# The last of 64 work units as eight block products, and closing sums moved to other places

## The chip, the cores and the metric

The kernel runs on one core of a Trainium2 chip. The metric is device time in microseconds (us) from start to end of one execution. The engines named below are PE (TensorE, matrix products into PSUM), DVE (VectorE), ACT (ScalarE), POOL (GpSimd) and SP (the engine that issues nearly all transfers). Each engine runs its own instructions strictly in program order and waits on semaphores for the others.

## The reference

```
def attention(q, k, v, p):                      # 8 batches, 8 heads, 576 tokens, width 64; p: 32 rows
    packed = softmax(p @ k.T / 8) @ v
    return softmax(q @ packed.T / 8) @ packed
x = attention(...).transpose(0, 2, 1, 3).reshape(4608, 512)
p = domain_probs / (domain_probs.sum(-1, keepdims=True) + 1e-9)
for e in range(4):                              # w1[e] 512x1024, w2[e] 1024x512, all fp32
    out += p[:, e:e+1] * (relu(x @ w1[e]) @ w2[e])
```

## The kernel before, in words

The second matrix product, `h @ w2`, is what this change is about. The 4 experts of 1024 hidden rows are cut into 8 chunks of 512, and the tokens into 8 batches of 576. One chunk of one batch is a unit: 64 units, counted here from 0. Batches go in pairs; within a pair the chunks go 0 to 7 and the two batches alternate, so unit 61 is chunk 6 of batch 7, unit 62 chunk 7 of batch 6 and unit 63, the last, chunk 7 of batch 7.

Within a unit the hidden block is a 2x2 matrix of blocks: a11, a12, a21, a22 (first digit token half, second digit hidden half), the weights are blocks b11 to b22 (hidden half, output half), and the product is formed in Winograd's way with seven block products instead of eight. `ORDER` lists their left operands, a11, s3, s1, s2, a22, s4, a12, where s1 to s4 are sums of the a blocks; the right operands (b11, b21, b22 and the sums t1 to t4) were formed once and are kept in DRAM (`td`), from which tiles `tt` come back. Every operand is split into a rounded high part and a low part, and a block product is 12 matmuls of 128x128 by 288 columns (`product`, L527): three of high and low for each of two hidden tiles and two output tiles. The first matmul of a product already reads the low part of its left operand.

- `mm1_group` (L414): four groups of 12 matmuls for each unit make the hidden blocks. DVE applies relu and the token weight, and builds s1 to s4 into tiles `sblk` and `ablk`.
- `s_operand` (L464): the split of a left operand into a tile `st` (4 buffers), two products ahead of its use: ACT casts the high part, POOL subtracts the low part. a12 is split by ACT and DVE into `stl`.
- `product`: its PSUM tile `dbl` is then added on DVE to one of seven accumulators `acc0` to `acc6` of the batch (the number is the place in `ORDER`); for chunk 0 ACT copies it.
- `combine` (L584), the closing sums of a batch: seven adds of accumulators, three on DVE, four on POOL, and four stores, one step after each product of the next unit. For the last batch `finish` (L556) does them instead, woven into unit 63's products, all on DVE.
- `g_form` (L370): in the first unit of a pair too, two PSUM tiles of matmuls (line L124) after product 0 make the weights of the next chunk (`ghl`), each tile emptied by two ACT casts and two DVE subtractions.

PSUM holds four `dbl` tiles, handed out in turn to products, groups and `g_form`. The order on TensorE is fixed by hand; the order on DVE, ACT, POOL and SP is chosen when the program is built, by a scheduler, within order constraints (`Behind`, L78, holds some DVE and POOL work behind other work). So the code's place of a step and its place in an engine's queue can differ.

Of the kernel before, what the change touches and what calls it, by code (L numbers as in the profile page):

```python
# [39 lines left out]
def attention_moe(ctx: ExitStack, tc: tile.TileContext, q, k, v, p, dp, w1, w2, out):  # L40
# [91 lines left out]
    def dbl():  # L132
        return ps_dbl.tile([P, 2, 512], F32, name="dbl")
# [15 lines left out]
    def hi_of(dst, src, eng):  # L149
        if eng in (nc.scalar, bact):  # L150
            return eng.copy(out=dst, in_=src)  # L151
        return eng.tensor_copy(out=dst, in_=src)

    def lo_of(dst, src, hi, eng):
        return eng.tensor_tensor(out=dst, in0=src, in1=hi.bitcast(F32), op=ALU.subtract)
# [255 lines left out]

    blocks = {}

    def mm1_group(u, kh, c):  # L414
        sb, ch, b = units[u]
        xh, xl = xs[b]
        ts = slice(c * HS, (c + 1) * HS)
        ps = dbl()
        for fi in range(2):
            f = 2 * kh + fi  # L420
            fs = slice(f * P, (f + 1) * P)
            n = 0
            for g in range(NG):
                ghl = gs[b, ch][g]
                for hl, rx in ((0, xl), (0, xh), (1, xh)):
                    mm(
                        out=ps[:, fi, 0:HS], lhsT=ghl[:, hl, fs], rhs=rx[:, g, c, 0:HS],
                        start=n == 0, stop=n == 3 * NG - 1,
                    )
                    n += 1  # L430
        psv = ps[:, :, 0:HS]

        def held(name):
            tag, bufs = ("ablk", 3) if name[0] == "a" else ("sblk", 4)
            blocks[u, name] = hpool.tile([P, 2, HS], F32, name=tag, bufs=bufs)
            return blocks[u, name]

        def add(dst, x, y, op):
            vec.tensor_tensor(out=dst, in0=x, in1=y, op=op)

        name = f"a{c + 1}{kh + 1}"
        vec.scalar_tensor_tensor(
            out=held(name) if c == kh else psv, in0=psv, scalar=0.0,
            in1=pbt[b][:, ts].rearrange("p (o t) -> p o t", o=1).broadcast_to([P, 2, HS]),
            op0=ALU.max, op1=ALU.mult,
        )
        if name == "a21":
            add(held("s3"), blocks[u, "a11"], psv, ALU.subtract)
            add(psv, psv, blocks[u, "a22"], ALU.add)
            add(held("s2"), psv, blocks[u, "a11"], ALU.subtract)  # L450
            nc.scalar.copy(out=held("s1"), in_=psv)  # L451
            if (u, "a12") in blocks:
                add(held("s4"), blocks[u, "a12"], blocks[u, "s2"], ALU.subtract)
        elif name == "a12":
            if (u, "s2") in blocks:
                add(held("s4"), psv, blocks[u, "s2"], ALU.subtract)
            else:
                blocks[u, "a12"] = psv
            st = hpool.tile([P, 2, 2, HP], F32R, name="stl")[:, :, :, 0:HS]
            hi_of(st[:, 0], psv, nc.scalar)  # L460
            lo_of(st[:, 1], psv, st[:, 0], vec)
            blocks[u, "op", NPROD - 1] = st

    def s_operand(u, i):  # L464

# [61 lines left out]
    def product(u, i):  # L527
        sb, ch, b = units[u]
        st, t = blocks.pop((u, "op", i)), tt[ch, i]
        ps = dbl()  # L530
        for j in range(2):
            n = 0
            for fi in range(2):
                for tl, sl in ((0, 1), (0, 0), (1, 0)):
                    mm(
                        out=ps[:, j, 0:HS], lhsT=t[:, tl, fi, j * P:(j + 1) * P], rhs=st[:, sl, fi, :],
                        start=n == 0, stop=n == 5,
                    )
                    n += 1
        order["product"] = order["free"][-1]  # L540
        psv = ps[:, :, 0:HS]
        if (b, i) not in accs:
            accs[b, i] = apool.tile([P, 2, HS], F32, name=f"acc{i}")
            nc.scalar.copy(out=accs[b, i], in_=psv)  # L544
        elif ch < NCH - 1 or b < B - 1:
            vacc.tensor_tensor(out=accs[b, i], in0=psv, in1=accs[b, i], op=ALU.add)
        else:
            finish(b, ORDER[i], psv)

    def store(b, t, r, n):  # L550
        nc.sync.dma_start(
            out=out[n * DH:(n + 1) * DH, b * S + r * HS:b * S + (r + 1) * HS].rearrange("(j p) t -> p j t", p=P),
            in_=t,
        )

    def finish(b, name, psv):  # L556

        m = {n: accs[b, i] for i, n in enumerate(ORDER)}

        def add(dst, x, y, op=ALU.add):  # L560
            vec.tensor_tensor(out=dst, in0=x, in1=y, op=op)

        t = m[name]
        if name == "a22":
            add(t, m["s3"], t, ALU.subtract)
            add(t, t, psv, ALU.subtract)
            store(b, t, 1, 0)
            return
        add(t, psv, t)
        if name == "a11":  # L570
            add(m["s2"], m["s2"], t)
            add(m["a12"], m["a12"], t)
        elif name == "s2":
            add(m["s3"], m["s3"], t)
            add(m["s4"], m["s4"], t)
            add(m["s4"], m["s4"], m["s1"])
            add(m["s1"], m["s1"], m["s3"])
            store(b, m["s1"], 1, 1)
        elif name == "s4":
            store(b, t, 0, 1)  # L580
        elif name == "a12":
            store(b, t, 0, 0)

    def combine(b):  # L584

        m = {n: accs[b, i] for i, n in enumerate(ORDER)}
        for eng, dst, x, y, op, to in (
            (cvec, "s2", "s2", "a11", ALU.add, None),
            (gq, "a12", "a12", "a11", ALU.add, (0, 0)),
            (cvec, "s3", "s3", "s2", ALU.add, None),  # L590
            (gq, "s4", "s4", "s1", ALU.add, None),
            (gq, "s4", "s4", "s2", ALU.add, (0, 1)),
            (cvec, "s1", "s1", "s3", ALU.add, (1, 1)),
            (gq, "a22", "s3", "a22", ALU.subtract, (1, 0)),
        ):
            eng.tensor_tensor(out=m[dst], in0=m[x], in1=m[y], op=op)
            if to is not None:
                store(b, m[dst], *to)
            yield

# [29 lines left out]
    def drain(gen):  # L630
        for _ in gen:
            pass
# [85 lines left out]
        w2_load(1, kh, raw_tile)  # L718
    tsteps = nothing
    kind = None  # L720
    sums, back = nothing, second_batch()
    for u, (sb, ch, b) in enumerate(units):
        pos = u % (2 * NCH)
        odd = pos % 2 == 1
# [21 lines left out]
        if fch is not None and u != 3 and not (u > 3 and odd):  # L746
            tsteps = t_form(fch)
        form_at = FORM.get(u, () if fch is None else (1, 2, 3, 4) if odd else (1, 4))
        for i in range(NPROD):
            product(u, i)  # L750
            n = i + LA
            if n < NPROD:
                s_operand(u, n)
            elif nxt:
                s_operand(u + 1, n - NPROD)
            if i in gat:
                if gat == (0,):
                    drain(gsteps)
                    if 0 < u < 4:
                        raws = w1_load({1: 0, 2: 2}[u])  # L760
                        if u == 2:
                            gsteps, gat = g_form([0, 1], 2, raws), (4, 5)
                else:
                    next(gsteps, None)
            if nxt:
                for grp in ((GROUPS_FIRST, GROUPS_LATE)[u] if u < 2 else GROUPS).get(i, ()):
                    mm1_group(u + 1, *grp)
            if i == 4 and 2 <= u < len(units) - 2 and units[u + 2][1] % 2 == 0:
                load_probs(units[u + 2][2], units[u + 2][1] // 2)
            if u == 0:  # L770
                next(back, None)
                next(back, None)
            elif i == 5 and kind != "scores" or i == 2 and u > 2 or i == 0 and odd and u > 3:
                kind = next(back, None)
            if i in form_at:
                next(tsteps, None)
            if u == 1 and i < 2:
                w2_load(2, i, raw_tile)
            if odd and u > 2 and fch is not None and fch + 1 < NCH and i in (3, 5):
                w2_load(fch + 1, i // 4, raw_tile)  # L780
            next(sums, None)
            if u < 2 or sb == 0 and u > 3 and not odd:
                t_store(ch, i)
            if u == 2:
                t_load(0, i)
            elif odd and nxt and not opening and fch is None:
                t_load(nxt[1], i)
        drain(gsteps)
        drain(sums)
        if ch == NCH - 1 and b < B - 1:  # L790
            sums = combine(b)
        if not odd and u > 0:
            nsb, nch = (sb, ch + 2) if ch + 2 < NCH else (sb + 1, ch + 2 - NCH)
            if nsb < SB:
# [35 lines left out]
```

## Time and profile before

| | us |
|---|---|
| median of 3 runs (1281.49 to 1284.88) | 1281.56 |
| the profiled execution | 1281.34 |
| its span in the trace | 1279.6 |
| PE busy | 1245.8 (97%) |
| DVE busy | 934.1 (73%) |
| POOL busy | 734.8 (57%) |
| ACT busy | 498.2 (39%) |

A busy share is a mean over the whole span. With PE at 97%, what a change off PE can be worth is read from the places where PE stands still, and from the stretch at the end in which PE has finished and others have not. Idle time in the rows stands in brackets with the engine and tile that ended it.

### The profile page before, as it was taken

The page shows a single profiled execution, that of the slowest core. Times are in us where ns is not written, and L with a number is a line of the kernel's source. Part 1 is how long each engine was busy: PE and PEld are TensorE (multiplying, and loading weights), DVE is VectorE, ACT ScalarE, POOL GpSimd, SP SyncE. Part 2 cuts the span into 40 slices and gives each one's busy share as a digit, 9 for nine tenths or more (in the row PEclk, how much of TensorE's full clock was granted, in tenths as well). Part 3 has the DMA queues.
Part 4 walks back from the last instruction along what each step waited for, and adds up shares of the span by engine and source line. Part 5 has one row for each costly group of instructions (what it writes and reads, how often), then busy time and mean ns, then how long its engine had stood idle before and what let it go on. Part 6 is the DMA issues. An engine that isn't in the chain of part 4 may idle for free.

```text
span 1279.6 us, 26886 instructions
## 1 busy us (share of the span) xinstructions
PE 1245.8 (97%) x10720; PEld 1165.0 (91%) x10720; DVE 934.1 (73%) x1398; ACT 498.2 (39%) x850; POOL 734.8 (57%) x528
## 2 busy tenths in 40 slices
PE   6899999999999999999999999999999999999996
PEld 3789899999999999999998999999999999999996
DVE  6676676888875677889776667788968466776667
ACT  3554544444445333334325434233334523332331
POOL 3876978798674434455566434454448544544554
PEclk9999999999999999999999999999999999999999
DMA  9765565545556444464444465433346443434322
GB/s 340 253 249 191 208 234 197 193 142 170 182 181 223 155 164 150 140 195 158 136 161 157 158 206 176 152 116 127 118 158 213 154 134 119 132 116 155 125 66 75
DMA packets 86219, 213.71 MB, mean 167 GB/s; under 512 B 8784, under 2 KB 27344, under 8 KB 86096
## 3 DMA queue, kind: packets, MB, share of 16 engines
q1 hardware_dynamic: 85424, 211.85, 49.6%
q8 instruction: 86, 1.41, 0.5%
q14 instruction: 37, 0.30, 0.1%
q10 hardware_dynamic: 672, 0.15, 0.1%
HBM read 173.09 MB, written 38.87 MB: 166 GB/s over the span
## 4 chain that ended last, share of the span: by engine, by line
PE 90%; DVE 4%; DMA 2%; POOL 2%; ACT 1%; issue 1%; DVEq 0%; SPq 0%; POOLq 0%; ACTq 0%
PE dbl L116 84%; PE dbl L124 5%; DVE acc L68 2%; DMA pnd<-ablk 1%; POOL st L68 1%; PE dbl L119 1%; DMA pbt<-pnd 1%; DVE a L68 1%; DVE sblk L68 0%; POOL tt L68 0%; DMA wraw<-in_w 0%; DVE dbl L68 0%; DVE ghl L68 0%; DMA rw<-in_w 0%; ACT st L151 0%
## 5 line engine op out<-in xcount | busy, mean ns | idle before, releaser
L116 PE MATMUL dbl<-st,tt 128*128 128x288 f32 x4608 | 666.4, 296 | 8.9 <-DVE ghl L68 5.1
L116 PEld LDWEIGHTS dbl<-st,tt 128*128 128x128 f32 x4608 | 623.1, 188 | 44.8 <-POOL st L68 24.8
L68 POOL TENSOR_TENSOR st<-sblk,st 128x576 fp32r<-128x576 f32 x256 | 370.0, 1456 | 447.4 <-ACT st L151 446.1
L116 PE MATMUL dbl<-xh,ghl 128*128 128x288 f32 x2048 | 413.6, 294 | 0.0
L68 DVE TENSOR_TENSOR acc<-dbl,acc 128x576 f32<-128x576 f32 x391 | 293.5, 752 | 87.9 <-PE dbl L116 85.5
L116 PEld LDWEIGHTS dbl<-xh,ghl 128*128 128x128 f32 x2048 | 328.2, 188 | 0.2 <-DVE ghl L68 0.2
L151 ACT CAST st<-sblk 128x576 fp32r<-128x576 f32 x256 | 166.7, 675 | 368.6 <-DVE sblk L68 296.7
L116 PE MATMUL dbl<-xl,ghl 128*128 128x288 f32 x1024 | 302.9, 296 | 6.0 <-POOL xl L68 5.7
L68 POOL TENSOR_TENSOR st<-ablk,st 128x576 fp32r<-128x576 f32 x128 | 188.6, 1473 | 45.4 <-ACT st L151 45.3
L116 PEld LDWEIGHTS dbl<-xl,ghl 128*128 128x128 f32 x1024 | 192.7, 188 | 8.8 <-POOL xl L68 6.4
L68 DVE SCALAR_TENSOR_TENSOR dbl<-dbl,pbt 128x576 f32<-128x576 f32 x128 | 97.8, 764 | 80.4 <-PE dbl L116 79.2
L68 DVE SCALAR_TENSOR_TENSOR ablk<-dbl,pbt 128x576 f32<-128x576 f32 x128 | 96.4, 753 | 67.7 <-PE dbl L116 65.2
L151 ACT CAST st<-ablk 128x576 fp32r<-128x576 f32 x128 | 86.3, 674 | 126.7 <-PE dbl L116 93.8
L116 PE MATMUL dbl<-stl,tt 128*128 128x288 f32 x768 | 113.0, 296 | 0.0
L116 PEld LDWEIGHTS dbl<-stl,tt 128*128 128x128 f32 x768 | 104.4, 188 | 0.2
L68 DVE TENSOR_TENSOR ghl<-dbl,ghl 128x512 fp32r<-128x512 f32 x128 | 84.9, 685 | 23.6 <-ACT ghl L151 23.6
L151 ACT CAST ghl<-dbl 128x512 fp32r<-128x512 f32 x128 | 72.3, 590 | 55.8 <-DVE ghl L68 54.8
L68 POOL TENSOR_TENSOR tt<-rw,tt 128x512 fp32r<-128x512 f32 x56 | 72.7, 1315 | 18.6 <-ACT tt L85 18.6
L68 DVE TENSOR_TENSOR stl<-dbl,stl 128x576 fp32r<-128x576 f32 x64 | 48.4, 756 | 39.1 <-ACT stl L151 39.1
L124 PE MATMUL dbl<-wraw,ppbd 64*32 64x512 f32 x1024 | 67.6, 595 | 0.9 <-DMA wraw<-in_w 0.9
L451 ACT COPY sblk<-dbl 128x576 f32<-128x576 f32 x64 | 41.1, 642 | 65.6 <-DVE sblk L68 65.6
L544 ACT COPY acc<-dbl 128x576 f32<-128x576 f32 x56 | 35.9, 642 | 51.8 <-PE dbl L116 49.1
(63 smaller groups left out, 703.4 us busy)
## 6 DMA issues: line engine op xcount, KB each, us to landing
tt<-td SPq DMA_DIRECT2D x175, 512.0 KB, 4.1
wraw<-in_w SPq DMA_DIRECT2D x132, 256.0 KB, 4.3
td<-tt SPq DMA_DIRECT2D x56, 512.0 KB, 5.2
pbt<-pnd SPq DMA_DIRECT2D x32, 288.0 KB, 3.8
out<-acc SPq DMA_DIRECT2D x32, 288.0 KB, 2.7
rw<-in_w SPq DMA_DIRECT2D x16, 512.0 KB, 5.7
kt<-in_k SPq DMA_DIRECT2D x14, 576.0 KB, 5.6
kt<-in_q SPq DMA_DIRECT2D x14, 576.0 KB, 5.4
```

The lines of the kernel that those rows point to most:

```text
L68: res = getattr(self.eng, op)(*args, **kw)
L116: on_pe(nc.tensor.matmul(**kw))
L119: on_pe(nc.tensor.transpose(**kw))
L124: ins = nc.tensor.matmul(**kw).ins
L151: return eng.copy(out=dst, in_=src)
L451: nc.scalar.copy(out=held("s1"), in_=psv)
L544: nc.scalar.copy(out=accs[b, i], in_=psv)
```

## The change

Unit 63 computes the eight plain block products (`last_unit`): for a11, a22, a21 and a12 in this order, two products each. The four PSUM tiles hold the four result blocks through the unit; the products of a11 and a22 open them and those of a21 and a12 add to them in PSUM. So unit 63 needs no s1 to s4: a21 and a12 are split straight from PSUM by ACT and DVE (`split`), a11 and a22 by `s_operand`. The eighth right operand, b12, is loaded and split once (`b12_load`, `b12_form`). The seven accumulators of batch 7 are combined after unit 61, in unit 62, and each result of unit 63 is then one add onto one accumulator and a store; the last one goes in two halves. `finish` is gone. The closing sums of batch 6 run beside unit 63. For batches 1, 3 and 5 the steps of `combine` come after products 2 to 5 of the next pair's first unit (two, two, two, one) instead of one after each product.

```
-        if name == "a21":
+        if u == len(units) - 1:
+            if c != kh:
+                split(u, name, psv)
+        elif name == "a21":
...
+    def b12_form(ch, raw):
+        t = wpool.tile([P, 2, 2, DH], F32R, name="tt", bufs=10)
+        hi_of(t[:, 0], raw, bact)
+        lo_of(t[:, 1], raw, t[:, 0], bpool)
+        tt[ch, "b12"] = t
...
+        for half, (left, r) in enumerate((("a11", 0), ("a22", 1), ("a21", 1), ("a12", 0))):
+            st = blocks.pop((u, "op", ORDER.index(left) if left in ORDER else left))
+            for n in range(2):
+                t = tt[ch, right[f"b{left[2]}{n + 1}"]]
+                if half < 2:
+                    pss[r, n] = dbl()
+                acc = accs[b, ORDER.index(RESULT[r, n])]
...
+                                rhs=st[:, sl, fi, :], start=half < 2 and k0 == 0, stop=half > 1 and k0 == 5,
...
+                parts = () if half < 2 else ((0, 1), (1, 2)) if (r, n) == (0, 1) else ((0, 2),)
+                for j0, j1 in parts:
+                    vacc.tensor_tensor(
+                        out=acc[:, j0:j1], in0=pss[r, n][:, j0:j1, 0:HS], in1=acc[:, j0:j1], op=ALU.add
+                    )
+                    store(b, acc[:, j0:j1], r, n, j0)
+                yield
...
+        if not nxt:
+            for _ in last_unit(u):
+                next(sums, None)
+            break
+        if u == len(units) - 2:
+            b12_form(ch, raw12)
...
-            next(sums, None)
+            for _ in range((0, 0, 2, 2, 2, 1, 0)[i] if late else 1):
+                next(sums, None)
...
-        if ch == NCH - 1 and b < B - 1:
-            sums = combine(b)
+        if ch == NCH - 1 and b < B - 1 or u == len(units) - 3:
+            sums, late = combine(b), b % 2 == 1 and b < B - 1
```

DVE's queue in the first unit of the second pair (before with -, now with +; `acc3` and `acc1` are accumulators of the batch that is closing, `ghl` the weights whose subtraction empties a PSUM tile):

```order
-L68 TENSOR_TENSOR acc3_1263<-acc3_1263,acc0_1164 128x576
 L68 TENSOR_TENSOR ghl_4707<-dbl_4689,ghl_4707 128x512
 L68 TENSOR_TENSOR ghl_4710<-dbl_4689,ghl_4710 128x512
-L68 TENSOR_TENSOR ghl_4732<-dbl_4690,ghl_4732 128x512
-L68 SCALAR_TENSOR_TENSOR ablk_4751<-dbl_4738,pbt_4604 128x576
+L68 TENSOR_TENSOR ghl_4731<-dbl_4690,ghl_4731 128x512
+L68 TENSOR_TENSOR ghl_4734<-dbl_4690,ghl_4734 128x512
+L68 SCALAR_TENSOR_TENSOR ablk_4750<-dbl_4737,pbt_4604 128x576
+L68 TENSOR_TENSOR acc3_1263<-acc3_1263,acc0_1164 128x576
+L68 SCALAR_TENSOR_TENSOR ablk_4804<-dbl_4791,pbt_4604 128x576
 L68 TENSOR_TENSOR acc1_1208<-acc1_1208,acc3_1263 128x576
-L68 TENSOR_TENSOR ghl_4735<-dbl_4690,ghl_4735 128x512
```

The first closing sum stood ahead of all four `ghl` and the second ahead of the last; both now stand behind all four. The other two boundaries between pairs change alike.

POOL's queue in units 62 and 63, before, from the low part of s3 of unit 62 to the last but one of unit 63 (`st` are low parts, `acc` closing sums of batch 6):

```order
L68 TENSOR_TENSOR st_15236<-sblk_15194,st_15236 128x2x288
L68 TENSOR_TENSOR st_15274<-sblk_15199,st_15274 128x2x288
L68 TENSOR_TENSOR st_15291<-sblk_15197,st_15291 128x2x288
L68 TENSOR_TENSOR st_15323<-ablk_15162,st_15323 128x2x288
L68 TENSOR_TENSOR st_15340<-sblk_15253,st_15340 128x2x288
L68 TENSOR_TENSOR st_15407<-ablk_15307,st_15407 128x2x288
L68 TENSOR_TENSOR st_15424<-sblk_15386,st_15424 128x2x288
L68 TENSOR_TENSOR acc5_12451<-acc5_12451,acc2_12360 128x576
L68 TENSOR_TENSOR acc6_12471<-acc6_12471,acc0_12276 128x576
L68 TENSOR_TENSOR st_15462<-sblk_15391,st_15462 128x2x288
L68 TENSOR_TENSOR st_15480<-sblk_15389,st_15480 128x2x288
L68 TENSOR_TENSOR st_15499<-ablk_15356,st_15499 128x2x288
```

And now, from the same low part of s3 to the first closing sum of batch 6 (`tt` is the low part of b12; `acc5_12666`, `acc6_12686` and `acc4_12628` belong to batch 7, `acc5_12453` to batch 6):

```order
L68 TENSOR_TENSOR st_15236<-sblk_15194,st_15236 128x2x288
L68 TENSOR_TENSOR tt_15262<-rw0_15260,tt_15262 128x512
L68 TENSOR_TENSOR acc5_12666<-acc5_12666,acc2_12573 128x576
L68 TENSOR_TENSOR acc6_12686<-acc6_12686,acc0_12518 128x576
L68 TENSOR_TENSOR st_15279<-sblk_15199,st_15279 128x2x288
L68 TENSOR_TENSOR st_15297<-sblk_15197,st_15297 128x2x288
L68 TENSOR_TENSOR st_15330<-ablk_15162,st_15330 128x2x288
L68 TENSOR_TENSOR st_15348<-sblk_15253,st_15348 128x2x288
L68 TENSOR_TENSOR acc5_12666<-acc5_12666,acc3_12593 128x576
L68 TENSOR_TENSOR acc4_12628<-acc1_12538,acc4_12628 128x576
L68 TENSOR_TENSOR st_15413<-ablk_15313,st_15413 128x2x288
L68 TENSOR_TENSOR acc5_12453<-acc5_12453,acc2_12357 128x576
```

Three operations more now stand ahead of the low part of s1 of unit 62 (`st_15279`), and two closing sums ahead of that of a11 of unit 63 (`st_15413`).

The last nine rows of DVE's queue before (each `dbl` is a product of unit 63, the other rows are `finish` and the last step of batch 6):

```order
L68 TENSOR_TENSOR acc1_12538<-acc1_12538,acc3_12593 128x576
L68 TENSOR_TENSOR acc5_12666<-acc5_12666,acc3_12593 128x576
L68 TENSOR_TENSOR acc4_12628<-acc1_12538,acc4_12628 128x576
L68 TENSOR_TENSOR acc5_12666<-acc5_12666,acc2_12573 128x576
L68 TENSOR_TENSOR acc4_12628<-acc4_12628,dbl_15526 128x576
L68 TENSOR_TENSOR acc2_12573<-acc2_12573,acc1_12538 128x576
L68 TENSOR_TENSOR acc5_12666<-dbl_15544,acc5_12666 128x576
L68 TENSOR_TENSOR acc2_12360<-acc2_12360,acc1_12319 128x576
L68 TENSOR_TENSOR acc6_12686<-dbl_15561,acc6_12686 128x576
```

And now, from the split of a12 of unit 63 (`stl`) to the end:

```order
L68 TENSOR_TENSOR stl_15448<-dbl_15434,stl_15448 128x2x288
L68 TENSOR_TENSOR acc3_12378<-acc3_12378,acc0_12276 128x576
L68 TENSOR_TENSOR acc1_12318<-acc1_12318,acc3_12378 128x576
L68 TENSOR_TENSOR acc4_12628<-dbl_15481,acc4_12628 128x576
L68 TENSOR_TENSOR acc2_12573<-dbl_15495,acc2_12573 128x576
L68 TENSOR_TENSOR acc2_12357<-acc2_12357,acc1_12318 128x576
L68 TENSOR_TENSOR acc6_12686<-dbl_15452,acc6_12686 128x576
L68 TENSOR_TENSOR acc5_12666<-dbl_15466,acc5_12666 128x288 x2
```

Behind the last matmul there now stand two adds of half the width, where a run of full-width adds stood. On SP, the transfer of b12 (256 KB, waiting for no engine) stands among the loads ahead of the first boundary, and the last store is two stores of half the size.

## Rows read from the trace of the kernel before

**Rows 1.** Waits of PE over the span: total us, times, longest us.

```profile
PE dbl L116 <- DVE ghl L68: 5.1, 4, 1.3
...
PE dbl L116 <- DVE stl L68: 1.4, 1, 1.4
...
PE dbl L116 <- POOL st L68: 0.3, 1, 0.3
```

**Rows 2.** PE at the first and last of three boundaries: start, us, what.

```profile
370.81 3.39 PE L116 MATMUL dbl<-st,tt 128*128 128x288 f32 x24 [1.29 <-DVE ghl L68]
...
988.28 3.40 PE L116 MATMUL dbl<-st,tt 128*128 128x288 f32 x24 [1.30 <-DVE ghl L68]
```

**Rows 3.** DVE in the first unit of the second pair.

```profile
366.78 1.82 DVE L68 TENSOR_TENSOR acc<-acc,acc 128x576 f32<-128x576 f32 x1
368.53 0.68 DVE L68 TENSOR_TENSOR ghl<-dbl,ghl 128x512 fp32r<-128x512 f32 x1
369.86 1.29 DVE L68 TENSOR_TENSOR ghl<-dbl,ghl 128x512 fp32r<-128x512 f32 x2 [0.65 <-ACT ghl L151]
...
371.73 1.82 DVE L68 TENSOR_TENSOR acc<-acc,acc 128x576 f32<-128x576 f32 x1
...
375.89 0.76 DVE L68 SCALAR_TENSOR_TENSOR ablk<-dbl,pbt 128x576 f32<-128x576 f32 x1 [1.74 <-PE dbl L116]
379.04 0.77 DVE L68 SCALAR_TENSOR_TENSOR dbl<-dbl,pbt 128x576 f32<-128x576 f32 x1 [2.39 <-PE dbl L116]
```

**Rows 4.** DVE and PE two units later, no closing sums.

```profile
406.54 0.68 DVE L68 TENSOR_TENSOR ghl<-dbl,ghl 128x512 fp32r<-128x512 f32 x1
...
407.87 1.29 DVE L68 TENSOR_TENSOR ghl<-dbl,ghl 128x512 fp32r<-128x512 f32 x2 [0.66 <-ACT ghl L151]
...
409.59 1.75 PE L116 MATMUL dbl<-st,tt 128*128 128x288 f32 x12
```

**Rows 5.** PE and DVE in units 62 and 63.

```profile
1244.12 3.32 PE L116 MATMUL dbl<-st,tt 128*128 128x288 f32 x24
...
1252.21 0.77 DVE L68 SCALAR_TENSOR_TENSOR dbl<-dbl,pbt 128x576 f32<-128x576 f32 x1 [0.82 <-PE dbl L116]
...
1256.76 3.32 PE L116 MATMUL dbl<-st,tt 128*128 128x288 f32 x24
```

**Rows 6.** POOL in units 62 and 63.

```profile
1237.32 1.44 POOL L68 TENSOR_TENSOR st<-sblk,st 128x576 fp32r<-128x576 f32 x1 [6.58 <-ACT st L151]
1240.03 2.83 POOL L68 TENSOR_TENSOR st<-sblk,st 128x576 fp32r<-128x576 f32 x2 [1.27 <-ACT st L151]
...
1254.70 1.44 POOL L68 TENSOR_TENSOR st<-sblk,st 128x576 fp32r<-128x576 f32 x1 [6.58 <-ACT st L151]
...
1262.20 1.95 POOL L68 TENSOR_TENSOR st<-ablk,st 128x576 fp32r<-128x576 f32 x1
```

**Rows 7.** The page's groups: POOL and ACT, count, busy us, mean ns.

```profile
L151 ACT CAST st<-sblk 128x576 fp32r<-128x576 f32 x256 | 166.7, 675 | 368.6 <-DVE sblk L68 296.7
...
L68 POOL TENSOR_TENSOR tt<-rw,tt 128x512 fp32r<-128x512 f32 x56 | 72.7, 1315 | 18.6 <-ACT tt L85 18.6
```

**Rows 8.** PE and DVE at the end.

```profile
1259.33 5.43 DVE L68 TENSOR_TENSOR acc<-acc,acc 128x576 f32<-128x576 f32 x3
...
1265.57 3.40 PE L116 MATMUL dbl<-st,tt 128*128 128x288 f32 x24 [1.44 <-DVE stl L68]
...
1268.81 1.75 PE L116 MATMUL dbl<-stl,tt 128*128 128x288 f32 x12
...
1274.76 0.74 DVE L68 TENSOR_TENSOR acc<-dbl,acc 128x576 f32<-128x576 f32 x1
```

**Rows 9.** Last stores: SP, and stores' time from issue to landing.

```profile
1272.86 3.04 SPq L551 DMA_DIRECT2D out<-acc  x5
...
DMA to landing us min/median/max: 2.2/2.7/5.7
```

**Rows 10.** Traffic from 1256 to 1279.6, in 40 slices of 0.59 us.

```profile
GB/s 0 0 0 0 0 0 150 340 10 0 0 0 0 0 0 0 0 0 0 28 14 344 143 0 160 334 6 0 0 0 301 355 350 348 340 350 363 94 0 0
```

More of the change, by code (lines that the diff above doesn't have):

```diff
@@ L412, in attention_moe, with split @@
     blocks = {}
+    def split(u, name, psv):
+        tag, bufs = ("stl", 1) if name == "a12" else ("st", 4)
+        st = hpool.tile([P, 2, 2, HP], F32R, name=tag, bufs=bufs)[:, :, :, 0:HS]
+        hi_of(st[:, 0], psv, nc.scalar)
+        lo_of(st[:, 1], psv, st[:, 0], vec)
+        blocks[u, "op", ORDER.index(name) if name in ORDER else name] = st
     def mm1_group(u, kh, c):
@@ L458, in mm1_group @@
                 blocks[u, "a12"] = psv
[L459 to L462, printed above, removed]
+            split(u, name, psv)
     def s_operand(u, i):
@@ L544, in product, with store @@
             nc.scalar.copy(out=accs[b, i], in_=psv)
-        elif ch < NCH - 1 or b < B - 1:
+        else:
             vacc.tensor_tensor(out=accs[b, i], in0=psv, in1=accs[b, i], op=ALU.add)
-        else:
-            finish(b, ORDER[i], psv)
-    def store(b, t, r, n):
+    def store(b, t, r, n, j0=0):
+        d0 = n * DH + j0 * P
         nc.sync.dma_start(
-            out=out[n * DH:(n + 1) * DH, b * S + r * HS:b * S + (r + 1) * HS].rearrange("(j p) t -> p j t", p=P),
+            out=out[d0:d0 + t.shape[1] * P, b * S + r * HS:b * S + (r + 1) * HS].rearrange("(j p) t -> p j t", p=P),
@@ L553, in store @@
             in_=t,
         )
[L556 to L582, printed above, removed]
+    RESULT = {(0, 0): "a12", (0, 1): "s4", (1, 0): "a22", (1, 1): "s1"}
@@ new lines, in b12_load, with last_unit @@
+    def b12_load(ch):
+        e, hf = divmod(ch, F // FC)
+        raw = raw_tile([P, 2, DH], "rw0")
+        nc.sync.dma_start(out=raw, in_=w2[e, hf * FC:hf * FC + 2 * P, DH:DM].rearrange("(f p) d -> p f d", p=P))
+        return raw
+    def b12_form(ch, raw):
[3 more added lines that the diff above has]
+        tt[ch, "b12"] = t
+    def last_unit(u):
+        sb, ch, b = units[u]
+        right = {"b11": ORDER.index("a11"), "b21": ORDER.index("a12"), "b22": ORDER.index("s4"), "b12": "b12"}
+        pss = {}
+        for half, (left, r) in enumerate((("a11", 0), ("a22", 1), ("a21", 1), ("a12", 0))):
[5 more added lines that the diff above has]
+                acc = accs[b, ORDER.index(RESULT[r, n])]
+                for j in range(2):
+                    k0 = 0
+                    for fi in range(2):
+                        for tl, sl in ((0, 1), (0, 0), (1, 0)):
+                            mm(
+                                out=pss[r, n][:, j, 0:HS], lhsT=t[:, tl, fi, j * P:(j + 1) * P],
+                                rhs=st[:, sl, fi, :], start=half < 2 and k0 == 0, stop=half > 1 and k0 == 5,
+                            )
+                            k0 += 1
+                order["product"] = order["free"][-1]
+                parts = () if half < 2 else ((0, 1), (1, 2)) if (r, n) == (0, 1) else ((0, 2),)
+                for j0, j1 in parts:
+                    vacc.tensor_tensor(
+                        out=acc[:, j0:j1], in0=pss[r, n][:, j0:j1, 0:HS], in1=acc[:, j0:j1], op=ALU.add
+                    )
+                    store(b, acc[:, j0:j1], r, n, j0)
+                yield
@@ L596, in combine @@
             eng.tensor_tensor(out=m[dst], in0=m[x], in1=m[y], op=op)
-            if to is not None:
+            if to is not None and b < B - 1:
                 store(b, m[dst], *to)
@@ L720, in attention_moe @@
     kind = None
-    sums, back = nothing, second_batch()
+    sums, late, back = nothing, False, second_batch()
     for u, (sb, ch, b) in enumerate(units):
@@ L753, in attention_moe @@
                 s_operand(u, n)
-            elif nxt:
-                s_operand(u + 1, n - NPROD)
+            else:
+                n -= NPROD
+                s_operand(u + 1, ORDER.index("a22") if n and u == len(units) - 2 else n)
             if i in gat:
@@ L785, in attention_moe @@
                 t_load(0, i)
-            elif odd and nxt and not opening and fch is None:
+            elif odd and not opening and fch is None:
                 t_load(nxt[1], i)
+        if u == len(units) - 3:
+            raw12 = b12_load(NCH - 1)
         drain(gsteps)
         drain(sums)
-        if ch == NCH - 1 and b < B - 1:
-            sums = combine(b)
+        if ch == NCH - 1 and b < B - 1 or u == len(units) - 3:
+            sums, late = combine(b), b % 2 == 1 and b < B - 1
         if not odd and u > 0:
```

## The prediction, made before the changed kernel ran

> **What bounds the kernel now.** I read the page's busy shares first: PE works for 97% of the span, so only two things can be won, time in which PE stands still and time after PE's last matmul. The waits of PE [rows 1] list the first. Four waits for `ghl` add up to 5.1 us. The timeline of PE puts three of them in the first unit of a pair, 1.29 us each (the first and the last of the three stand in [rows 2]), and the fourth (5.1 - 3 x 1.29 = 1.2 us) in an early unit that the change leaves alone. A wait for `stl` (1.4) and short ones for `st` lie in unit 63. Then I read DVE, POOL and PE beside each other at the boundary [rows 3] and in an undisturbed unit [rows 4], and the last two units [rows 5, 6, 8]. PE ends at 1268.81 + 1.75 = 1270.56, DVE at 1274.76 + 0.74 = 1275.50, and the span at 1279.6: nine microseconds at the end in which PE has nothing to do, over half of them DVE's adds, the rest the last stores.
>
> **The boundaries between pairs (three times).** At 366.78 DVE begins the first closing sum. It takes 1.82 us, where an add that reads PSUM takes 0.74 [rows 3, 8]. Only then comes the first `ghl` (368.53), and the second, which empties the PSUM tile, runs at 369.86 + 0.65 = 370.5; PE starts its next product at 370.81, 1.29 late [rows 2]. In the changed queue the sum stands behind all four `ghl`. The first can start at 366.8, 1.73 earlier, the second ends near 368.8, and PE was ready at 370.81 - 1.29 = 369.52. The unit without closing sums shows this order: second `ghl` done at 407.87 + 0.65 = 408.5, PE on the product at 409.59, no wait [rows 4]. So the stall goes: 3 x 1.29 = -3.87 us.
>
> What is late next there? The first sum would now run from about 371.4 to 373.2, the second behind the next relu. The relu after the first sum waited for PE and started at 375.89, which becomes 374.6 when PE comes 1.29 earlier: 1.4 us after the sum's end. The one after the second sum starts at 379.04 - 1.29 = 377.75 [rows 3], and the sum ends near 374.6 + 0.75 + 1.82 = 377.1: 0.6 to spare. I count nothing for either. On POOL two closing sums move behind one low part each; that only brings the low parts forward. SP's order of stores and loads there is unchanged. The load of b12, 256 KB, joins SP's queue near the first boundary and waits for no engine: nothing. Bounds for a boundary: nothing won (0), or 1.29 each.
>
> **Unit 62.** POOL now has b12's low part and two closing sums of batch 7 ahead of s1's low part. It is free at 1237.32 + 1.44 = 1238.76 [rows 6]. b12's low part costs 1.32 [rows 7]; back to back POOL needs 2.83 / 2 = 1.42 for an operation [rows 6]. So s1's low part ends at 1238.76 + 1.32 + 3 x 1.42 = 1244.34, and PE's product wanted it at 1244.12 [rows 5]: 0.27 late with the signal. The s2 part is wanted one product later. A product adds 3.32 - 1.75 = 1.57 us (24 matmuls [rows 5] less twelve [rows 4, 8]). If DVE's closing sum comes between, a POOL operation takes 1.95 instead of 1.43 [rows 6], s2 ends at 1246.28 and PE loses another 0.36. I take 0.6 together; ends 0.2 (POOL never disturbed) and 2.2 (all at 1.95). The low parts behind have room: before, POOL stood idle for 6.58 us ahead of 1254.70 [rows 6]. ACT's cast for b12 (0.6) falls in a gap of 1.3 us there.
>
> **Unit 63.** Its first product is at 1256.76 in the old time [rows 5], 1257.36 with the 0.6. It needs a11's low part. On ACT the casts of a11 and a22 now stand behind that of a21, which waits for the relu of a21 (1252.21 + 0.77, plus 0.6: 1253.6 [rows 5]). Two casts of 0.675 [rows 7] and a low part of 1.44 to 1.95 give 1256.4 to 1256.9: in time by half a microsecond or more. The fourth PSUM tile is freed by the split of a12: relu, cast and subtraction (0.77 + 0.68 + 0.74) behind one closing sum and one add on DVE, near 1260.5, wanted at 1257.36 + 3 x 1.57 = 1262.1. The operands of the second half are older still. So I expect eight products without a stall: 1257.36 + 7 x 1.57 + 1.75 = 1270.10. Before, seven without a stall would have ended at 1256.76 + 6 x 1.57 + 1.75 = 1267.93; they ended at 1270.56. The eighth product costs 1.57 and unit 62 costs 0.6, the old stalls give back 2.63: PE ends 0.5 earlier. Ends: 0.8 earlier to 1.5 later.
>
> **After PE.** Nothing but two half adds is left. The trace has 0.74 for 576 columns and 0.68 for 512 [rows 8, 3], about 1 ns a column, so 288 columns take about 0.47; two with the signal end near 1270.1 + 1.0 = 1271.1, against 1275.50. The other adds of unit 63 come one per product (1.57 apart, each 0.74, one of them a closing sum of up to 1.82), so none is left over.
>
> The stores: before, five were issued from 1272.86 to 1275.90 [rows 9], each 295 KB, and the traffic stood at 340 to 363 GB/s until about 1278.4 [rows 10]: five take 5 x 295 / 350 = 4.2 us, so they queued. From the last byte to the span's end were 1.2. Now the last stores are 1.6 us apart and the last two half as large; the fastest landing of a full store is 2.2 after its issue [rows 9], so I take 2.0 for the half one (1.8 to 2.7): 1271.1 + 2.0 + 1.2 = 1274.3. The end of the span moves by 1274.3 - 1279.6 = -5.3 us.
>
> The Trainium skill ("DMA: Bandwidth & Descriptors", Anatomy of one DMA) gives each transfer a fixed cost of about 2.0 us plus its bytes at 436 GB/s, a fit for transfers issued from GpSimd. By it halving the last store saves only 0.34, the store lands after 2.34, and the sum would be 0.34 worse, 1272.7 by an estimate from that page. For the full store it gives 2.68: the median of the rows, 2.7, agrees, their fastest, 2.2, does not.
>
> **The sum.** -3.87 - 5.3 = -9.2 us, from the profiled execution's 1281.34 to 1272.2. The median shown is 0.22 above that execution, so I forecast 1272.4.
>
> **Rivals.**
> *The boundary stalls stay.* PE's wait is put down to the event that came last; if PE is held there by something else, for instance the chain by which ACT's next `ghl` cast waits for DVE, the order of the sums changes little. For it: the casts and subtractions alternate [rows 3]. Against it: rows 4 have the same alternation without a wait. Time: 1272.4 + 3.9 = 1276.3.
>
> *Unit 62 hangs on POOL.* POOL gets five more operations there, while DVE does three closing sums. If all run at 1.95, s1's part ends at 1238.76 + 1.32 + 3 x 1.95 = 1245.9, PE loses 1.8 and some 0.4 at s2; a11's part adds up to 1. Time: 1274 to 1275.5. For it: the slow durations appear wherever both close sums [rows 6, 8]. Against it: the first two closing sums of POOL start before DVE's first.
>
> *The moved sums hold PE at the boundary.* Both sums now stand ahead of a relu whose result frees a PSUM tile, in a unit where PE comes earlier. If PE waited for both in full (2 x 1.82 = 3.64), three boundaries would cost 10.9 instead of giving 3.87: 1272.4 + 3.87 + 10.9 = 1287.2, slower than before. It decides once a sum is late by more than DVE's spare time, 0.6 and 1.4 us as worked out above; it turns the total to slower from about 3 us for each boundary. For it: sums that wait for POOL last 1.82, and POOL is busy there. Against it: DVE's idle 1.74 and 2.39 before these relus.
>
> **How the numbers follow.** A difference within 0.3% (3.8 us) can't be told from no change here, so faster means under 1277.7. Forecast 0.72 (its own range 1270.8 to 1274, from the ends of unit 62, the store and PE's end); stalls stay 0.10; POOL in unit 62 0.14; sums hold PE 0.04. The first counts as faster in full, the second for 0.06 and else as same, the third for 0.12. Faster 0.90, same 0.06, slower 0.04. The range goes from 1270.6, a little more won at the store, to 1276.8, which takes in the second and third case.
>
> **What would show it.** Right: no PE wait for `ghl` near 369.5, 677 and 984; a wait of a few tenths for `st` at the third product of unit 62; unit 63 one run of 96 matmuls; DVE done within 1 us of PE; the last store landing some 2 us later. Wrong: waits of over 1 us at these boundaries, PE waits in unit 63 for `st` or `stl`, or stores of batch 6 still moving when the last one is issued.

## The result, and the profile after

The changed kernel takes 1272.59 us, median of 4 runs (1270.89 to 1272.88), against 1282.15 of the kernel before (1281.49 to 1284.88). The ratio is 0.9919, 95% interval [0.9901, 0.9936]: faster, by 9.6 us by the medians. The forecast was 1272.4, range 1270.6 to 1276.8. The profiled execution took 1272.35, its span is 1270.6.

The start of the kernel varies from run to run: the first boundary between pairs comes at 366.10 in the profile before and at 367.42 in the one after. That is not the change: the fifth experiment below, which has it too, comes there at 366.20, and the first, which differs from the kernel before only from there on, at 367.71. So the parts are read as distances within one trace. The waits of PE after, those of the products' line (total us, times, longest us), to be held against [rows 1]:

```profile
PE dbl L116 <- POOL xl L68: 5.7, 1, 5.7
...
PE dbl L116 <- DVE acc L68: 1.8, 1, 1.8
PE dbl L116 <- POOL st L68: 1.5, 1, 1.5
...
PE dbl L116 <- ACT at L85: 1.0, 1, 1.0
```

`ghl` and `stl` are gone from the list; the four waits that are left lie in the first 140 us. The 1.5 for `st` is not new: it is the fourth wait of [rows 1], in the early unit (1.22 us at 136.82 before, 1.52 at 138.13 after), only put down to another engine. The boundary, timeline of PE (product 1 before; then products 1 and 2 of the pair's first unit after) and of DVE after, against [rows 2, 3]:

```profile
366.10 1.84 PE L116 MATMUL dbl<-st,tt 128*128 128x288 f32 x12
```

```profile
367.42 1.85 PE L116 MATMUL dbl<-st,tt 128*128 128x288 f32 x12
370.68 3.32 PE L116 MATMUL dbl<-st,tt 128*128 128x288 f32 x24
```

```profile
368.11 0.68 DVE L68 TENSOR_TENSOR ghl<-dbl,ghl 128x512 fp32r<-128x512 f32 x1
369.44 1.29 DVE L68 TENSOR_TENSOR ghl<-dbl,ghl 128x512 fp32r<-128x512 f32 x2 [0.65 <-ACT ghl L151]
371.38 0.69 DVE L68 TENSOR_TENSOR ghl<-dbl,ghl 128x512 fp32r<-128x512 f32 x1 [0.65 <-ACT ghl L151]
371.99 0.75 DVE L68 SCALAR_TENSOR_TENSOR ablk<-dbl,pbt 128x576 f32<-128x576 f32 x1
372.65 1.94 DVE L68 TENSOR_TENSOR acc<-acc,acc 128x576 f32<-128x576 f32 x1
375.69 0.76 DVE L68 SCALAR_TENSOR_TENSOR ablk<-dbl,pbt 128x576 f32<-128x576 f32 x1 [1.10 <-PE dbl L116]
376.37 1.80 DVE L68 TENSOR_TENSOR acc<-acc,acc 128x576 f32<-128x576 f32 x1
378.85 0.77 DVE L68 SCALAR_TENSOR_TENSOR dbl<-dbl,pbt 128x576 f32<-128x576 f32 x1 [0.68 <-PE dbl L116]
```

Products 1 and 2 start 370.68 - 367.42 = 3.26 apart, without a wait; before it was 370.81 - 366.10 = 4.71. The sums still take 1.8 to 1.9 us, now between relus that wait for PE anyway (1.10 and 0.68 left).

PE in unit 62 before (products 0 and 1, and 4):

```profile
1239.38 3.32 PE L116 MATMUL dbl<-st,tt 128*128 128x288 f32 x24
...
1248.86 1.74 PE L116 MATMUL dbl<-st,tt 128*128 128x288 f32 x12
```

Units 62 and 63 after, PE (products 0 and 1, then 2 and 3, then 4 of unit 62; the 96 matmuls of unit 63) and POOL, against [rows 5, 6]:

```profile
1236.13 3.32 PE L116 MATMUL dbl<-st,tt 128*128 128x288 f32 x24
...
1241.01 3.75 PE L116 MATMUL dbl<-st,tt 128*128 128x288 f32 x24
...
1246.18 1.74 PE L116 MATMUL dbl<-st,tt 128*128 128x288 f32 x12
...
1254.08 9.64 PE L116 MATMUL dbl<-st,tt 128*128 128x288 f32 x72
1263.56 3.32 PE L116 MATMUL dbl<-stl,tt 128*128 128x288 f32 x24
```

```profile
1234.08 1.44 POOL L68 TENSOR_TENSOR st<-sblk,st 128x576 fp32r<-128x576 f32 x1 [6.58 <-ACT st L151]
1235.47 1.30 POOL L68 TENSOR_TENSOR tt<-rw,tt 128x512 fp32r<-128x512 f32 x1
1236.73 2.83 POOL L68 TENSOR_TENSOR acc<-acc,acc 128x576 f32<-128x576 f32 x2
1239.52 3.34 POOL L68 TENSOR_TENSOR st<-sblk,st 128x576 fp32r<-128x576 f32 x2
...
1251.68 1.43 POOL L68 TENSOR_TENSOR st<-ablk,st 128x576 fp32r<-128x576 f32 x1 [2.74 <-ACT st L151]
```

From product 0 to product 4 of unit 62 are 10.05 us, 0.57 more than before (1248.86 - 1239.38 = 9.48). Product 2 starts 4.88 behind product 0 instead of 4.74 [rows 5], so it is 0.14 late; the other 0.43 lie between products 2 and 3 (3.75 for the two instead of 3.32), where no row of waits names them. Unit 63 is 1263.56 + 3.32 - 1254.08 = 12.80 us without a gap; seven products took 13.80 before. The end, DVE and SP, against [rows 8 to 10]:

```profile
1262.24 0.76 DVE L68 TENSOR_TENSOR acc<-dbl,acc 128x576 f32<-128x576 f32 x1 [3.03 <-PE dbl L116]
...
1266.91 0.82 DVE L68 TENSOR_TENSOR acc<-dbl,acc 128x288 f32<-128x288 f32 x2 [0.82 <-PE dbl L116]
```

```profile
out<-acc SPq DMA_DIRECT2D x2, 144.0 KB, 1.8
```

```profile
1257.84 10.39 SPq L558 DMA_DIRECT2D out<-acc  x9
```

The second view has the two half stores, with the time from issue to landing. PE ends at 1266.88, DVE at 1267.73, SP has issued the last store at 1268.23, and the span ends at 1270.6: 3.72 us behind PE, where it was 1279.6 - 1270.56 = 9.04.

| distance within one trace, us | before | after | change | forecast |
|---|---|---|---|---|
| products 1 to 2 at a boundary, three times | 4.71 | 3.26 | 3 x -1.45 = -4.35 | -3.87 |
| unit 62, product 0 to 4 | 9.48 | 10.05 | +0.57 | +0.6 |
| unit 63, PE | 13.80 | 12.80 | -1.00 | -1.06 |
| PE's end to the span's end | 9.04 | 3.72 | -5.32 | -4.84 |
| sum | | | -10.1 | -9.2 |

The spans differ by less, 1279.6 - 1270.6 = 9.0, because the first boundary comes 1.3 later in the trace after.

### The profile page after: what moved, and what is told of

Same layout as the page of the kernel before. It is cut to its first block, busy times and chain, and to the rows that moved or that the text cites. A ratio compares the mean times of both kernels' runs of the same rounds, so it can differ in the third digit from the quotient of the medians.

```text
span 1270.6 us, 26902 instructions
## 1 busy us (share of the span) xinstructions
PE 1247.0 (98%) x10732; PEld 1166.7 (92%) x10732; DVE 926.1 (73%) x1389; ACT 496.1 (39%) x847; POOL 735.8 (58%) x529
## 4 chain that ended last, share of the span: by engine, by line
PE 91%; POOL 2%; DMA 2%; DVE 2%; issue 1%; ACT 0%; SPq 0%; DVEq 0%; POOLq 0%; ACTq 0%
PE dbl L116 85%; PE dbl L124 6%; POOL st L68 1%; DMA rw<-in_w 1%; PE dbl L119 1%; DMA pbt<-pnd 1%; DMA vt<-in_v 1%; DVE a L68 1%; POOL tt L68 1%; POOL acc L68 0%; DVE dbl L68 0%; DVE sblk L68 0%; DVE s L68 0%; POOL rw L68 0%; ACT st L151 0%
## 5 line engine op out<-in xcount | busy, mean ns | idle before, releaser
L68 POOL TENSOR_TENSOR st<-sblk,st 128x576 fp32r<-128x576 f32 x252 | 364.7, 1458 | 435.9 <-ACT st L151 434.6
L151 ACT CAST st<-sblk 128x576 fp32r<-128x576 f32 x252 | 164.1, 675 | 362.6 <-DVE sblk L68 290.9
```

The source lines that it names most:

```text
L68: res = getattr(self.eng, op)(*args, **kw)
```

## The experiments

**The moved sums alone.**

```
 (kernel before)
-    sums, back = nothing, second_batch()
+    sums, late, back = nothing, False, second_batch()
...
-            next(sums, None)
+            for _ in range((0, 0, 2, 2, 2, 1, 0)[i] if late else 1):
+                next(sums, None)
...
-            sums = combine(b)
+            sums, late = combine(b), b % 2 == 1
```

> The kernel before with one thing changed: the closing sums of batches 1, 3 and 5 come after products 2 to 5 of the next pair's first unit. If the 1.3 us waits at the boundaries come from the closing sum that stands ahead of the ghl subtractions on DVE, PE has no wait for ghl there, its products 1 and 2 start 3.26 us apart instead of 4.71, and the time falls by 3 x 1.45 = 4.35, to about 1277.8 (0.9966); the last unit stays as before (PE waits 1.4 for stl, DVE done 4.9 after PE). If PE is held there by something else, 4.71 stays and the time is 1282.

1277.95 us (1276.53 to 1278.34), ratio 0.9954 [0.994, 0.9968]. PE at the boundary and in unit 63:

```profile
367.71 1.85 PE L116 MATMUL dbl<-st,tt 128*128 128x288 f32 x12
370.98 3.32 PE L116 MATMUL dbl<-st,tt 128*128 128x288 f32 x24
...
1257.38 3.76 PE L116 MATMUL dbl<-st,tt 128*128 128x288 f32 x24 [0.30 <-POOL st L68]
1262.57 3.40 PE L116 MATMUL dbl<-st,tt 128*128 128x288 f32 x24 [1.44 <-DVE stl L68]
```

3.27 apart at the boundary, and the waits of unit 63 are those of before. Moving the sums is what removes the wait.

**The last unit alone.**

```
 (kernel after)
-            for _ in range((0, 0, 2, 2, 2, 1, 0)[i] if late else 1):
-                next(sums, None)
+            next(sums, None)
```

> The changed kernel with the closing sums of batches 1, 3 and 5 back at one after each product. If the two parts are independent, the three waits of 1.3 us are back, the end is as in the changed kernel (12.8 us of PE for unit 63, DVE done 0.9 after PE), and the time is 1272.6 + 4.35 = 1276.9. If the gain was all in the last unit, 1272.6.

1276.92 us (1276.14 to 1278.74), ratio 0.9952 [0.994, 0.9965]. The wait is back at all three boundaries (the first and last of them):

```profile
371.86 3.40 PE L116 MATMUL dbl<-st,tt 128*128 128x288 f32 x24 [1.29 <-DVE ghl L68]
...
989.39 0.89 PE L116 MATMUL dbl<-st,tt 128*128 128x288 f32 x5 [1.29 <-DVE ghl L68]
```

The end is that of the changed kernel (unit 63 in 12.80, 3.66 behind PE). Beside the kernel before of the same series (1282.84) the two parts give 4.9 and 5.9 us, 10.8 together; the whole change gave 9.6 by medians. Within the intervals the parts add up, and neither needs the other.

**The last store whole.**

```
-                parts = () if half < 2 else ((0, 1), (1, 2)) if (r, n) == (0, 1) else ((0, 2),)
+                parts = () if half < 2 else ((0, 2),)
```

> The changed kernel with the last result added and stored in one piece. One add of 0.76 instead of two that take 0.82 together, one issue of 0.39 less on SP, but the last transfer twice as long (0.42 more). If the transfer decides, the span from PE's last matmul to the end grows by 0.2 to 0.4; if the second issue decides, it shrinks by up to 0.4. Time within 0.4 of 1272.6 either way; the profile has to tell.

1272.28 us (1271.52 to 1273.42), ratio 0.9915 [0.9901, 0.9929]: by times no difference. The end in the trace, PE, DVE and the last store alone:

```profile
1263.86 3.32 PE L116 MATMUL dbl<-stl,tt 128*128 128x288 f32 x24
1267.22 0.76 DVE L68 TENSOR_TENSOR acc<-dbl,acc 128x576 f32<-128x576 f32 x1 [0.82 <-PE dbl L116]
```

```profile
DMA to landing us min/median/max: 2.2/2.2/2.2
```

PE ends at 1267.18, DVE at 1267.98, and the span at 1271.6: 4.42 behind PE, where the halves have 3.72. Of these 0.7 us the transfer accounts for 0.4, as expected: the whole store lands 2.2 after its issue, a half 1.8. The second issue costs under 0.1: SP issues the second half 0.12 after DVE has done it, the whole store 0.03 after. The rest lies behind the landing: it comes at 1268.0 + 2.2 = 1270.2, and the span ends 1.4 later, where it is 0.95 with halves. What sets these last microseconds no run shows, so only 0.4 are the halves' by this trace, and the times do not show even that.

**Closing sums of batch 7 behind the low parts.**

```
+        gsum = bpool if b == B - 1 else gq
...
-            (gq, "a12", "a12", "a11", ALU.add, (0, 0)),
+            (gsum, "a12", "a12", "a11", ALU.add, (0, 0)),
...
-            for _ in range((0, 0, 2, 2, 2, 1, 0)[i] if late else 1):
+            for _ in range((0, 0, 2, 2, 2, 1, 0)[i] if late else (0, 0, 0, 3, 2, 1, 1)[i] if u == len(units) - 2 else 1):
```

`gsum` stands in place of `gq` in all four sums on POOL; it holds those of batch 7 behind the low parts.

> The changed kernel with the closing sums of batch 7 behind product 3 of unit 62, on POOL behind the low parts of s1, s2, a22 and s4. If the 0.57 us that PE loses at products 2 and 3 of unit 62 come from the two sums ahead of s1's low part and DVE's sum between, products 0 and 2 start 4.74 apart and product 2 and the next group 3.16, and the time falls by 0.57 to 1272.0, as long as the later sums hold up no operand of unit 63. If the low part of b12 alone makes it, PE still waits 0.1 or more. If the sums now hold a11's low part, a wait ahead of unit 63 of up to 1 us.

1271.54 us (1270.68 to 1272.0), ratio 0.9908 [0.9894, 0.9921]. PE in unit 62 and POOL in unit 63:

```profile
1235.87 3.32 PE L116 MATMUL dbl<-st,tt 128*128 128x288 f32 x24
...
1240.61 3.32 PE L116 MATMUL dbl<-st,tt 128*128 128x288 f32 x24
...
1245.35 1.74 PE L116 MATMUL dbl<-st,tt 128*128 128x288 f32 x12
```

```profile
1255.98 6.65 POOL L68 TENSOR_TENSOR acc<-acc,acc 128x576 f32<-128x576 f32 x4
```

9.48 from product 0 to 4: the 0.57 are gone, with b12's low part still in its place. But the four sums of batch 6 now run in a row on POOL until 1262.63, the stores of batch 6 come later, and the traffic of the last 20 us (40 slices of 0.5 us) shows the stores queued:

```profile
GB/s 0 0 0 0 0 0 0 0 0 0 0 0 0 0 0 0 0 0 0 33 177 339 44 18 271 323 16 319 362 353 328 367 342 353 355 339 349 41 0 16
```

The end is 4.05 behind PE (PE 1266.05, span 1270.1) instead of 3.72, and the last half store lands 2.1 after its issue instead of 1.8: 0.33 of the 0.57 is given back there. I had not expected that.

**Closing sums one product sooner.**

```
-            for _ in range((0, 0, 2, 2, 2, 1, 0)[i] if late else 1):
+            for _ in range((0, 2, 2, 2, 1, 0, 0)[i] if late else 1):
```

> The changed kernel with the closing sums of batches 1, 3 and 5 one product sooner (after products 1 to 4: two, two, two, one). On DVE the first two sums now stand behind all four ghl but together ahead of the next relu, 3.7 us where about 3 are free, so that relu comes 0.7 us late at three boundaries. If PE needs nothing from that relu until later (its tile is taken up again four products on), no PE wait and the time stays at 1272.6. If the sums ahead of the relu hold PE, as the third rival had it, 0.7 or more at each boundary: 1274.7 or more.

1272.2 us (1271.15 to 1274.04), ratio 0.9921 [0.9909, 0.9934], and 3.26 between products 1 and 2. DVE at the boundary:

```profile
371.43 2.72 DVE L68 TENSOR_TENSOR acc<-acc,acc 128x576 f32<-128x576 f32 x2
374.47 0.76 DVE L68 SCALAR_TENSOR_TENSOR ablk<-dbl,pbt 128x576 f32<-128x576 f32 x1 [0.32 <-PE dbl L116]
```

The two sums take 2.72 together, not 3.7 as expected, and the relu still waits for PE by 0.32. The case of a relu that comes late did not arise, so this shows only that the sums fit there, not what a late relu would cost.

**Accumulators not combined one unit sooner.**

```
-        if ch == NCH - 1 and b < B - 1 or u == len(units) - 3:
+        if ch == NCH - 1 and b < B - 1:
...
+            sums = chain(combine(b), sums)
             for _ in last_unit(u):
                 next(sums, None)
+                next(sums, None)
```

> The changed kernel with the accumulators of batch 7 not combined one unit sooner: their closing sums run in unit 63 with those of batch 6, two steps after each product. Two of the POOL sums still go early by the scheduler's choice, so unit 62 loses the same 0.57. If the earlier combining is what makes the end short, POOL and DVE now have more sums to do behind the first results: DVE's and POOL's last sums and the stores of batch 6 come 2 to 4 us later and the end grows by 1 to 3 us, to 1273.6 to 1275.6. If eight products in PSUM alone are enough, 1272.6.

1273.77 us (1273.41 to 1278.1), ratio 0.994 [0.9926, 0.9953]. PE in unit 62 (products 0 and 1, 2 and 3, 4) and at the end, and DVE in unit 63:

```profile
1235.68 3.32 PE L116 MATMUL dbl<-st,tt 128*128 128x288 f32 x24
...
1240.56 3.42 PE L116 MATMUL dbl<-st,tt 128*128 128x288 f32 x24
...
1245.40 1.74 PE L116 MATMUL dbl<-st,tt 128*128 128x288 f32 x12
...
1262.78 3.33 PE L116 MATMUL dbl<-stl,tt 128*128 128x288 f32 x24
```

```profile
1255.70 5.90 DVE L68 TENSOR_TENSOR acc<-acc,acc 128x576 f32<-128x576 f32 x4
1262.92 0.76 DVE L68 TENSOR_TENSOR acc<-dbl,acc 128x576 f32<-128x576 f32 x1 [1.32 <-POOL acc L68]
```

The first result now waits for POOL's sum instead of PE, the stores bunch up, and the span ends 5.49 behind PE (PE 1266.11): 1.77 more than after. The same 0.57 was expected for unit 62, but it loses only 0.24 (9.72 from product 0 to 4): POOL's two sums still stand ahead of s1's low part, while DVE's sum no longer falls between the low parts, which take 2.84 for two instead of 3.34. So 0.24 of the 0.57 go with POOL's sums and 0.33 with DVE's. Of the 5.32 us at the end, 3.55 come with eight products in PSUM alone and 1.77 with the earlier combining, for this order of the sums: batch 7's stood ahead of batch 6's, and the other order was not run.

**Closing sums of batch 7 between the low parts** (the edit of the fourth experiment with another row of steps).

```
-            for _ in range(... else (0, 0, 0, 3, 2, 1, 1)[i] if u == len(units) - 2 else 1):
+            for _ in range(... else (0, 2, 2, 2, 1, 0, 0)[i] if u == len(units) - 2 else 1):
```

> The changed kernel with the closing sums of batch 7 spread over products 1 to 4 of unit 62 and on POOL behind the low part due then: s1 and s2 first, then a sum, a22, a sum, s4, two sums. If the 0.57 us of unit 62 come from the sums ahead of s1's low part, they go as with all sums behind s4, and if the stores of batch 6 were what lengthened the end there (4.05 us from PE's last matmul against 3.72), the end is back at 3.7: 1272.6 - 0.57 = 1272.0. If the sum by DVE now hits another low part, up to 0.4 comes back.

1271.08 us (1270.42 to 1271.86), ratio 0.9914 [0.99, 0.9927]. PE in unit 62:

```profile
1234.81 3.32 PE L116 MATMUL dbl<-st,tt 128*128 128x288 f32 x24
...
1244.29 1.74 PE L116 MATMUL dbl<-st,tt 128*128 128x288 f32 x12
```

9.48 again, and the end 3.71 behind PE (PE 1264.99, span 1268.7). Both halves of the reading of the fourth experiment hold: the 0.57 go when the low parts of s1 and s2 come ahead of all sums of batch 7, on POOL and on DVE, and the 0.33 go with them when the stores of batch 6 do not come late. It has the least median of all kernels that ran, but by the intervals of the ratios it can't be told from the changed kernel.

## Why the prediction was right

The mechanisms held in all four places. That the time came within 0.2 us of the forecast is in part luck: the parts gave 10.1 us where 9.2 were forecast, and the start of the kernel alone varies by more than that difference.

**The boundaries.** The step held: the closing sum stood ahead of the subtraction that empties a PSUM tile, and behind it nothing waits. The first two experiments show it from both sides. The size was off: -4.35 where I had -3.87. The 1.29 in brackets counts idle time from the end of the matmul before, which the profile models; the distance of the starts, 4.71 against 3.26, gives 1.45. The rival that PE is held by something else is out.

**Unit 62.** 0.57 where I had 0.6, by the operations named: s1's low part late behind POOL's sums, s2's by DVE's sum. The fourth and the last experiment remove it, the sixth separates the two. The terms were less exact than their sum: product 2 is 0.14 late where I had 0.27, product 3 another 0.43 where I had 0.36. The wait of a few tenths that I named as a sign stands in no row of waits; it shows in the starts alone. The rival that the unit hangs on POOL by 2 us or more did not come: of the four low parts (s1, s2, a22, s4), POOL's long form (1.9 instead of 1.4) hit two.

**Unit 63.** 12.80 for eight products without a gap, 12.74 forecast. a11's low part was done at 1251.68 + 1.43 = 1253.11, 1.0 us before its product at 1254.08: the earlier end of what I had (1256.4 against 1257.36).

**After PE.** DVE was done 0.85 after PE, forecast 1.0. From DVE's end to the span's end were 2.87 us, forecast 3.2: the half store landed 1.8 after its issue began (1268.23 - 0.38 = 1267.85) where I had taken 2.0, and the span ended 0.95 behind that landing where I had 1.2. That the stores queued before, five in a row at 350 GB/s, is borne out where they bunch up again: in the fourth experiment the last half store lands after 2.1, in the sixth the last three after 2.6 to 3.0. The Trainium skill ("DMA: Bandwidth & Descriptors", Anatomy of one DMA) gives a fixed cost of about 2.0 us, fitted to transfers issued from GpSimd. This whole transfer, issued from SP, took 1.8, so the estimate of 2.34 for the half store by the Trainium skill is too long here; its estimate of 0.34 saved by halving fits, since the whole store of the third experiment landed after 2.2 and a half after 1.8. The median of 2.7 [rows 9], which agreed with 2.68, takes in stores that queued.

**The slower rival**, sums that hold PE at the boundary, did not come: 1.10 and 0.68 us were left on DVE, 1.4 and 0.6 forecast, and still 0.32 in the fifth experiment. What a late relu would cost stays open.

## What to carry to other kernels

A small wait of the bound engine that recurs at seams is worth tracing to the one foreign instruction ahead of the release; moving that instruction behind it cost nothing here. At the end of a kernel, more work for the bound engine can be the cheaper way when it shortens what follows its last instruction: 1.6 us for an eighth product bought 5.3 us at the end, a third of which came from combining one unit sooner, in the order tried. Work moved into such a unit needs a place behind the operands that are due first, and stores that come late queue behind one another (0.33 us in the fourth experiment).

## What the runs showed of the hardware that was not expected

An idle time in brackets on PE was shorter than what its removal gave back (1.29 against 1.45), since the profile models the end of a matmul: the distance of the starts is the safer reading.

A closing sum on DVE, an add of two SBUF operands, took 1.8 to 1.9 us when it began during an operation of POOL [rows 3], and 0.76 when POOL stood idle. The two sums of the fifth experiment show both (ns, shortest, median, longest), with POOL beside them:

```profile
L68 DVE TENSOR_TENSOR acc<-acc,acc x2: 759/1344/1930, 371.4 to 373.4; 128x576 f32<-128x576 f32 x2
```

```profile
371.31 1.43 POOL L68 TENSOR_TENSOR st<-sblk,st 128x576 fp32r<-128x576 f32 x1 [1.82 <-ACT st L151]
373.50 3.86 POOL L68 TENSOR_TENSOR acc<-acc,acc 128x576 f32<-128x576 f32 x2 [0.76 <-DVE acc L68]
```

The first sum took 1.93 beside POOL's operation, which ended at 372.74; the second, from 373.4 on, took 0.76. That is why the two together took 2.72 and not 3.7, while three in a row beside a busy POOL took 5.43 in the kernel before [rows 8]. It is a reading of traces; no run changed POOL's work alone.
